# Second expert layer's weight tiles divided into four and three products, with buffers for each, in a fused attention and two-layer kernel

## The chip, the cores and the metric

The kernel runs on one core of a Trainium2 chip. The metric is the device time of one execution in microseconds (us), lower is better. Three runs of the kernel before are shown, and one further execution was profiled.

## The reference, cut to what matters

Causal attention with a bias from cumulative sums, then two expert layers. The second of these is the one the change touches: `x` is 2304 tokens of 512 numbers, `w_in` 512 x 2048, `w_out` 2048 x 512.

```python
attn_out = _attn_ref(q, k, v, s)                    # 4 batches, 8 heads, 576 tokens, 64 wide
x = attn_out.transpose(0, 2, 1, 3).reshape(B * S, H * D)
x = (x @ w_a) * (x @ w_b) @ w_out                   # first expert layer, 512 -> 1536 -> 512
h = x @ w_in                                        # second expert layer
r = np.maximum(h, 0.0)
return (r * r) @ w_out
```

## The kernel before

**Order.** Python code traces the whole program as operations with costs and dependences, and the class `Plan` (lines 73 to 261) sorts them: it keeps a clock for each engine and for the DMA queue and gives each engine the operation that can start first, ties by a rank. A tile's buffers belong to a tag with a fixed count (`Tag`); a tile can start when a buffer of its tag is free. So a change of tags or sizes in one place moves operations of every engine from the first point on at which such a tile matters. All operations are issued at line 261 (line 256 for fillers), so the trace is read by tile names, not by lines. All loads and stores are issued by SP, in the planned order; a DMA that waits holds up those behind it on SP.

**Numbers.** Each matrix product of 32-bit numbers is made of three matmuls: a high part (`..h`) times high, low times high, high times low. A tile pair (`z` = 0, 1) holds high and low words of a weight.

**Stages.** Attention and the first expert layer run together until about 380 us; the first layer then goes on by chunks (tiles `ab`, `py`), and its last chunk of 768 tokens, `wide` (lines 1174 to 1314, tiles `wa`, `wb`, `wc`, `pw`), uses seven products of 2 x 2 blocks in place of eight. The second layer works that way throughout: for each of three groups of 768 tokens (`t0`) and each of eight pairs of blocks (`j`, `PAIRS`) `first` (lines 1351 to 1426) makes the seven products, named `b11`, `b21`, `b22`, `t1` to `t4`, each six matmuls of 128 x 384, in the banks `a`, `b` and `c` (tiles `pa`, `pb`, `pc`). Its order is b11 in bank a, b21 in b, t2 onto a, t1 in c, t3 onto a, t4 onto a, b22 onto c. Between the products that add onto bank a ScalarE copies the bank out (`keep`, tiles `1..`, `2..`, `3..`, the copy before t2, t3, t4). `second` (lines 1448 to 1537, tiles `po`) multiplies the squares with the second matrix's tiles `ws` of 512 KB; the planner mixes both.

**The weights of `first`.** `split_in` (line 931) prepares seven combinations of the first matrix for each pair `j` and stores them to DRAM as `w2q[j][z]`, 128 rows of seven words of `QW` = 256 numbers, in the order of `SEVEN` (line 867). `first` loads both tiles whole, 896 KB each, and `times` picks a product's word by its place in `SEVEN`:

```python
def block(nm):
    return gated("lop", [P, 7, QW], F32R, "wq", 4, nm)
...
w = [block(f"w{nm}_{z}") for z in range(2)]
for z in range(2):
    dma(w[z].rearrange("p q c -> p (q c)").bitcast(F32), w2q[j][z], 896)
```

The tag `wq` has four buffers of 7168 bytes per partition, two pairs' worth. The same tag lends its first 4096 bytes to the sums `ws` of `wide` (line 1196) and, at the very end, to four of the seven last tiles `ws` of `second` (line 1455, products t3, t2, t4, b21 of `ENDING`); the other last tiles, b11, b22 and t1, use the three buffers of tag `lo`.

Of the kernel before, what the change touches and what calls it, by code (L numbers as in the profile page):

```python
# [7 lines left out]
F32 = mybir.dt.float32  # L8
F32R = mybir.dt.float32r
# [7 lines left out]
P = 128  # L17
# [246 lines left out]
def attention_moe_moe(tc, q, k, v, s, w_a, w_b, w_out, w_in2, w_out2, out):  # L264
    nc = tc.nc
    B, H, D, S = q.shape
    DM, NT = out.shape
# [33 lines left out]
    pl = Plan(nc)  # L301
# [15 lines left out]
    def pool(name):  # L317
        return lambda: pools[name]

    def gated(name, shape, dtype, tag, bufs, nm):  # L320
        return pl.tile(pool(name), shape, dtype, tag, bufs, nm, swapped)

    def sb(shape, dtype, tag, bufs, name):
        return pl.tile(pool("sb"), shape, dtype, tag, bufs, name)
# [4 lines left out]
    def scratch(shape, dtype, name):  # L329
        return pl.fixed(lambda: pools["dram"].tile(shape, dtype, name=name))  # L330

    def mm_bank(name):
        return pl.tile(pool("mm"), [P, 512], F32, "mm", 3, name)
# [5 lines left out]
    def matmul(out, n, pairs, start=True, lag=0.0):  # L339
        more = {} if start else {"skip_group_check": True}  # L340
        calls = [
            ("matmul", (out, a, b), {"start": start and i == 0, "stop": i == len(pairs) - 1, **more})
            for i, (a, b) in enumerate(pairs)
        ]
        cost = len(pairs) * (n / 2.4 + 13)
        pe(cost, calls, out, [x for pair in pairs for x in pair], lag)
# [19 lines left out]
    def dma(out, in_, kb, takes=(), lag=0.0):  # L366
        pl.call(("SP", kb * 3.0, False, "dma_start", (out, in_), {}), takes=takes, lag=lag)
# [496 lines left out]

    PAIRS = NF2 // 2
    QW = 2 * P
    SEVEN = ["b11", "b21", "t4", "t2", "b22", "t3", "t1"]
    w2q = [[scratch([P, 7 * QW], F32, f"w2q{j}_{z}") for z in range(2)] for j in range(PAIRS)]

    def temp(dtype, nm):  # L870
        return gated("lop", [P, 2 * DM], dtype, "tmp", 4, nm)

    def block(nm):
        return gated("lop", [P, 7, QW], F32R, "wq", 4, nm)

    def combine(n, out, a, b, op=ALU.subtract):
        kw = {"out": out, "in0": a, "in1": b, "op": op}
        pl.call(on_gps("tensor_tensor", n, **kw), on_dve("tensor_tensor", n, two=True, **kw))
# [52 lines left out]
    def split_in(j, late=False):  # L931
        def send(j, names, both):
            l, n = SEVEN.index(names[0]), len(names) * QW
            for z, x in enumerate(both):
                dma(w2q[j][z][:, l * QW : l * QW + n].part(names[0]), x.bitcast(F32), 0.6 * n)
# [58 lines left out]
    def halves(nm, dtype):  # L994
        t = sb([P, 2 * W], dtype, "g", GB, nm)
        return [t[:, z * W : z * W + W].part(z) for z in range(2)]
# [164 lines left out]
    def product(ps, left, right, start=True):  # L1161
        xh, xl = right
        pairs = []
        for d in range(2):
            wh_, wl_ = (z[d] for z in left)
            pairs += [(wh_, xh[:, d]), (wh_, xl[:, d]), (wl_, xh[:, d])]
        matmul(ps, CW, pairs, start, 0.0 if start else STEP)
# [6 lines left out]
    def wide(c):  # L1174
# [17 lines left out]
        def sums(f):  # L1192
            nm = f"{c}_{f}"
            lo = sb([P, 2, ND, P], F32R, "lo", 3, f"lo{nm}")
            dma(lo.bitcast(F32), wlab[f], 512)
            ws = gated("lop", [P, 7 * QW], F32, "wq", 4, f"ws{nm}")[:, : 2 * DM]
            a11, a12, a21, a22 = (ws[:, i * QW : i * QW + QW].part(i // 2) for i in range(4))
            for i in range(2):
                combine(
                    DM, ws[:, i * DM : i * DM + DM].part(i), wh[f, i].rearrange("p d c -> p (d c)").bitcast(F32),  # L1200
                    lo[:, i].rearrange("p d c -> p (d c)").bitcast(F32), ALU.add,
                )
            combine(QW, a22, a21, a22, ALU.add)
            combine(QW, a21, a11, a21)
            combine(QW, a11, a22, a11)
            combine(QW, a12, a12, a11)
            left[f] = lo, ws
# [84 lines left out]
        for f in range(3):  # L1292
            sums(f)
# [42 lines left out]
    def urgent(f, *a, **kw):  # L1336
        was, pl.stream = pl.stream, "first"
        f(*a, **kw)
        pl.stream = was
# [11 lines left out]
    def first(t0, j, left, held):  # L1351

        nm = f"{t0}_{j}"
        pair = j % 2
        yq = y_quads[t0]
        w = [block(f"w{nm}_{z}") for z in range(2)]
        for z in range(2):
            dma(w[z].rearrange("p q c -> p (q c)").bitcast(F32), w2q[j][z], 896)

        def times(ps, q, start=True):  # L1360
            i = SEVEN.index(q)
            product(ps, [[x[:, i, d * P : d * P + P] for d in range(2)] for x in w], yq[q], start)

        def bank_(k):
            if t0 == 0 and j == 1:
                return gated("po", [P, 512], F32, "po", 5, f"p{k}{nm}")[:, :CW]
            return mm_bank(f"p{k}{nm}")[:, :CW]

        v1, v3 = (x[:, :CW] for x in halves(f"v{nm}a", F32))
        v2, v4 = (x[:, :CW] for x in halves(f"v{nm}b", F32))  # L1370

        def squared(v, ps, s):
            if s is None:
                urgent(act, "activation", CW, v, ps, AF.Relu, psum=True)
            else:
                urgent(dve, "tensor_tensor", CW, out=v, in0=ps, in1=s, op=ALU.add)
                pl.call(
                    on_act("activation", CW, v, v, AF.Relu),
                    on_dve("tensor_scalar_max", CW, v, v, 0.0, two=True, each=0.52),
                )  # L1380
            kw = {"out": v, "in0": v, "in1": v, "op": ALU.mult}
            pl.call(on_act("activation", CW, v, v, AF.Square), on_dve("tensor_tensor", CW, two=True, **kw))
            return v

        def split(q, v):
            if q in ROOM:
                if pair == 0:
                    held[q] = flat(ROOM[q], 1, f"g{nm}{q}")
                hi, lo = (held[q][:, 2 * pair + z, :CW].part((pair, z)) for z in range(2))
            else:  # L1390
                hi, lo = (flat("wh", 3 * NF1, f"g{nm}{q}{z}")[:, :CW] for z in range(2))
            left[q, pair] = hi, lo
            copy(CW, hi, v, by="A")
            subtract(CW, lo, v, hi.bitcast(F32))

        def keep(tag, bufs, width, k, ps):
            t = sb([P, width], F32, tag, bufs, f"{k}{nm}")[:, :CW]
            urgent(act, "copy", CW, t, ps, psum=True)
            return t

        a = bank_("a")
        times(a, "b11")
        s1 = keep("a", 2, 512, 1, a)
        b = bank_("b")
        times(b, "b21")
        b11 = squared(v1, b, s1)
        times(a, "t2", False)
        s2 = keep("lo1", 1, DM, 2, a)
        b = bank_("c")
        times(b, "t1")  # L1410
        times(a, "t3", False)
        s3 = keep("a", 2, 512, 3, a)
        b22 = squared(v3, b, s3)
        times(a, "t4", False)
        b21 = squared(v2, a, None)
        times(b, "b22", False)
        b12 = squared(v4, b, s2)
        split("b11", b11)
        split("b22", b22)
        split("b21", b21)  # L1420
        combine(CW, b22, b22, b12)
        combine(CW, b12, b12, b11)
        combine(CW, b11, b11, b22, ALU.add)
        combine(CW, b21, b21, b11)
        for q, v in (("t3", b22), ("t1", b12), ("t2", b11), ("t4", b21)):
            split(q, v)
# [21 lines left out]
    def second(t0, grp, left, q, d):  # L1448

        nm = f"{t0}_{grp}{q}"  # L1450
        last = grp == PAIRS // 2 - 1
        end = last and t0 + 2 * CW >= NT
        if d == 0:
            if end and ENDING.index(q) > 2:
                wt = block(f"ws{nm}")[:, :4].rearrange("p (a b) c -> p a b c", a=2)
            else:
                wt = sb([P, 2, 2, QW], F32R, "lo", 3, f"ws{nm}")
            streamed[nm] = wt
            src = w2s[grp][OUT.index(q)]
            pl.add(  # L1460
                {"SP": (1536.0, [("dma_start", (wt.bitcast(F32), src), {})], False)},
                [wt], [src.part((q, i, z)) for i in range(2) for z in range(2)],
            )
        wt = streamed[nm]
        stays = q in STAYS
        if not stays:
            ps = mm_bank(f"po{nm}{d}") if end and (ENDING.index(q) + d) % 2 else gated("po", [P, 512], F32, "po", 5, f"po{nm}{d}")
        elif grp == 0:
            if (q, d) == (STAYS[0], 0):
                ps = mm_bank(f"po{nm}{d}")  # L1470
            else:
                ps = gated("po", [P, 512], F32, "po", 5, f"po{nm}{d}")
            banks_[q, d] = ps
        else:
            ps = banks_[q, d]
        ps = ps[:, :CW]
# [14 lines left out]
        x = {k: (lambda k: lambda: home(t0, k, d))(k) for k in ORDER}  # L1491
# [108 lines left out]
```

## Time and profile before

| | |
|---|---|
| median of 3 runs | 1021.84 us (1020.78 to 1024.65) |
| profiled execution, its own time | 1023.91 us |
| its span in the trace | 1022.1 us |
| TensorE matmuls busy | 1002.8 us, 98% |
| VectorE, ScalarE, GpSimd busy | 72%, 59%, 32% |
| DMA | 240.58 MB, mean 235 GB/s |
| loads of `w` | 48 of 896 KB, median 6.7 us to landing |

How to read it: a busy share near 100% on one engine means that only what lets that engine stand still can move the time. PE is TensorE's matmuls, PEld its weight loads, DVE VectorE, ACT ScalarE, POOL GpSimd, SP the engine that issues the DMAs. Idle time is read as the length of a stretch less the busy time in it, and the list of waits tells which instruction ended it.

### The profile page before, as it was taken

How to read it: one execution, taken by the hardware profiler on the slowest of the kernel's cores; microseconds unless marked ns; L12 is line 12 of the kernel's file. 1: busy time of each engine (PE TensorE's matmuls, PEld its weight loads, DVE VectorE, ACT ScalarE, POOL GpSimd, SP SyncE). 2: the span in 40 equal slices, each digit the busy share in tenths (PEclk: the TensorE clock that was granted, in tenths of full speed). 3: DMA queues.
4: the chain of work that ended last, by engine and by line, in shares of the span. 5: the costliest groups of instructions: out<-in, count | busy, mean ns of one | idle time of the engine just before them, and what ended most of it. 6: DMA issues, size and time to landing. Idle time of an engine off the chain costs nothing.

```text
span 1022.1 us, 16764 instructions
## 1 busy us (share of the span) xinstructions
PE 1002.8 (98%) x5612; PEld 867.8 (85%) x5619; DVE 735.5 (72%) x1546; ACT 603.9 (59%) x1373; POOL 322.3 (32%) x293
## 2 busy tenths in 40 slices
PE   9999999999999999999999999999999999999997
PEld 5766777777777778788889999999999999999997
DVE  5878876756677765565697898688767755876566
ACT  6777886565777643343344544487565766657552
POOL 2243134325454622101122323323335212431123
PEclk9999999999999999999999999999999999999999
DMA  7458896558778667857666668499968876678664
GB/s 226 131 157 256 273 288 186 152 150 258 228 199 246 185 212 262 275 183 233 206 207 207 208 206 273 164 336 363 344 219 322 313 260 231 246 273 319 220 233 165
DMA packets 138006, 240.58 MB, mean 235 GB/s; under 512 B 21320, under 2 KB 91072, under 8 KB 137920
## 3 DMA queue, kind: packets, MB, share of 16 engines
q1 hardware_dynamic: 137920, 239.52, 71.1%
q8 instruction: 44, 0.72, 0.3%
q14 instruction: 42, 0.34, 0.1%
HBM read 181.42 MB, written 52.11 MB: 228 GB/s over the span
## 4 chain that ended last, share of the span: by engine, by line
PE 75%; DMA 5%; DVE 2%; SPq 1%; ACT 1%; issue 0%; DVEq 0%; ACTq 0%
PE ab L261 14%; PE pa L261 9%; PE py L261 8%; PE po_0t L261 6%; PE pw L261 5%; PE pc L261 5%; PE wa L261 4%; PE st L261 3%; PE av L261 3%; PE pt L261 3%; PE wc L261 2%; PE pb L261 2%; PE po_2b L261 2%; PE po_1b L261 2%; PE po_0b L261 2%; PE po_3b L261 2%
## 5 line engine op out<-in xcount | busy, mean ns | idle before, releaser
L261 ACT ACTIVATE e<-st,neg 120x336 f32<-120x336 f32 (+2 forms) x192 | 93.5, 492 | 28.5 <-DVE neg L261 26.6
L261 PE MATMUL py<-g,wh 128*128 128x512 f32 x288 | 92.0, 401 | 1.4 <-DVE y L261 1.2
L261 PE MATMUL ab<-xh,wh 128*128 128x512 f32 x192 | 77.4, 403 | 0.0
L261 PE MATMUL ab<-xh,lo 128*128 128x512 f32 x192 | 75.0, 391 | 0.0
L261 PE MATMUL ab<-xl,wh 128*128 128x512 f32 x192 | 75.0, 390 | 0.0
L261 PE MATMUL pt<-ident,e 120*120 120x120 f32 (+2 forms) x480 | 68.0, 268 | 0.8 <-DVE ph L261 0.4
L261 PEld LDWEIGHTS pt<-ident,e 120*120 120x120 f32 (+2 forms) x480 | 51.2, 133 | 20.2 <-issue 9.2
L261 DVE CUSTOM_DVE_ANT_0 st<-st,mask 96x96 f32<-96x96 f32 (+4 forms) x120 | 53.7, 453 | 20.0 <-PE st L261 18.2
L261 PE MATMUL ab<-x,wh 128*128 128x512 f32 x192 | 65.8, 424 | 0.8 <-ACT a L261 0.7
L261 PEld LDWEIGHTS py<-g,wh 128*128 128x128 f32 x288 | 53.3, 190 | 12.6 <-DVE y L261 1.6
L261 PE MATMUL av<-ph,val 120*64 120x240 f32 (+3 forms) x512 | 58.7, 360 | 0.0
L261 PE MATMUL st<-fk,fq 65*120 65x336 f32 (+2 forms) x192 | 56.3, 408 | 1.7 <-ACT e L261 1.7
L261 ACT COPY ph<-pt 120x360 f32<-120x360 f32 (+3 forms) x81 | 36.5, 459 | 35.9 <-PE pt L261 34.8
L261 PE MATMUL py<-g,loo 128*128 128x512 f32 x144 | 56.9, 395 | 0.0
L261 PEld LDWEIGHTS av<-ph,val 120*64 120x64 f32 (+1 forms) x512 | 31.1, 136 | 24.9 <-issue 12.4
L261 DVE COPY ph<-pt 120x360 f32<-120x360 f32 (+3 forms) x79 | 39.8, 514 | 16.2 <-PE pt L261 14.9
L261 DVE TENSOR_TENSOR ab<-ab,a 128x512 f32<-128x512 f32 x36 | 25.2, 701 | 33.3 <-PE ab L261 28.7
L261 PEld LDWEIGHTS ab<-xh,lo 128*128 128x128 f32 x192 | 36.0, 188 | 7.7
L261 ACT COPY a<-ab 128x512 f32<-128x512 f32 x36 | 21.1, 586 | 35.7 <-PE ab L261 35.6
L261 PEld LDWEIGHTS ab<-xh,wh 128*128 128x128 f32 x192 | 36.1, 188 | 6.4 <-issue 0.4
L261 PEld LDWEIGHTS ab<-x,wh 128*128 128x128 f32 x192 | 33.7, 189 | 9.2 <-ACT a L261 1.6
L261 PEld LDWEIGHTS ab<-xl,wh 128*128 128x128 f32 x192 | 36.2, 188 | 5.9
(692 smaller groups left out, 3098.4 us busy)
## 6 DMA issues: line engine op xcount, KB each, us to landing
w<-w2q SPq DMA_DIRECT2D x48, 896.0 KB, 6.7
lo<-wlab SPq DMA_DIRECT2D x36, 512.0 KB, 4.7
w2q<-w2ip SPq DMA_DIRECT2D x48, 256.0 KB, 4.2
w2s<-w2op SPq DMA_DIRECT2D x48, 256.0 KB, 4.6
loo<-wlo SPq DMA_DIRECT2D x24, 384.0 KB, 5.5
w2ir<-in_moe_w_in SPq DMA_DIRECT2D x16, 512.0 KB, 5.7
w2or<-in_moe_w_out SPq DMA_DIRECT2D x16, 512.0 KB, 4.3
ws_0t<-w2s SPq DMA_DIRECT2D x12, 512.0 KB
```

Source lines behind the costliest of these rows:

```text
L261: getattr(eng, method)(*map(real, args), **{k: real(a) for k, a in kw.items()})
```

## The change

`SEVEN` is put in another order: b11, b21, t3, t1, then t4, t2, b22. A `w` tile is no longer loaded whole: words 0 to 3 go into a tile of tag `wq4` (512 KB), words 4 to 6 into one of tag `wq3` (384 KB), each tag with four buffers, together as many bytes as before. `times` takes its word from the half that holds it. The sums of `wide` and the last tiles of `second` use `wq4`. There are 96 loads of `w` in place of 48, and each waits only for the stores of its own words. The number and shapes of the matmuls stay.

```diff
-    SEVEN = ["b11", "b21", "t4", "t2", "b22", "t3", "t1"]
+    SEVEN = ["b11", "b21", "t3", "t1", "t4", "t2", "b22"]
+    NEAR = 4
...
-    def block(nm):
-        return gated("lop", [P, 7, QW], F32R, "wq", 4, nm)
+    def block(nm, n=NEAR):
+        return gated("lop", [P, n, QW], F32R, f"wq{n}", 4, nm)
...
-            ws = gated("lop", [P, 7 * QW], F32, "wq", 4, f"ws{nm}")[:, : 2 * DM]
+            ws = gated("lop", [P, 2 * DM], F32, f"wq{NEAR}", 4, f"ws{nm}")
...
-        w = [block(f"w{nm}_{z}") for z in range(2)]
-        for z in range(2):
-            dma(w[z].rearrange("p q c -> p (q c)").bitcast(F32), w2q[j][z], 896)
+        w = {}
+        for c0, n in ((0, NEAR), (NEAR, 7 - NEAR)):
+            for z in range(2):
+                w[c0, z] = block(f"w{nm}_{c0}{z}", n)
+                src = w2q[j][z][:, c0 * QW : (c0 + n) * QW]
+                pl.add(
+                    {"SP": (n * 384.0, [("dma_start", (w[c0, z].rearrange("p q c -> p (q c)").bitcast(F32), src), {})], False)},
+                    [w[c0, z]], [src.part(x) for x in ("b11", "t3", "t4", "t2") if c0 <= SEVEN.index(x) < c0 + n],
+                )
...
             i = SEVEN.index(q)
-            product(ps, [[x[:, i, d * P : d * P + P] for d in range(2)] for x in w], yq[q], start)
+            c0 = i // NEAR * NEAR
+            product(ps, [[w[c0, z][:, i - c0, d * P : d * P + P] for d in range(2)] for z in range(2)], yq[q], start)
...
-                wt = block(f"ws{nm}")[:, :4].rearrange("p (a b) c -> p a b c", a=2)
+                wt = block(f"ws{nm}").rearrange("p (a b) c -> p a b c", a=2)
```

In the rows below a name like `w_3_1` is pair 3, low words; in the change `w_3_01` is pair 3, words from 0, low, and `w_3_40` words from 4, high; the last number is the tile's own.

SP, the loads of pairs 2 and 3 for the first 768 tokens (`yd` stores the first layer's result, `ws_0b` are weights of `second`). Before:

```order
L261 DMA w_2_0_7358<-w2q_0_3969 128x1792
L261 DMA w_2_1_7364<-w2q_1_3997 128x1792
L261 DMA yd_7274<-yo_3_7402 128x512
L261 DMA yd_7274<-yo_4_7425 128x256
L261 DMA ws_0b_7445<-w2s_5673 128x1024
L261 DMA yd_7274<-yo_4_7425 128x256
L261 DMA yd_7274<-yo_5_7440 128x256 x2
L261 DMA w_3_0_7484<-w2q_0_4504 128x1792
L261 DMA w_3_1_7487<-w2q_1_4517 128x1792
```

The change:

```order
L261 DMA w_2_00_7349<-w2q_0_3969 128x1024
L261 DMA w_2_01_7358<-w2q_1_3997 128x1024
L261 DMA yd_7287<-yo_3_7368 128x512
L261 DMA w_2_40_7390<-w2q_0_3969 128x768
L261 DMA w_2_41_7395<-w2q_1_3997 128x768
L261 DMA ws_0b_7412<-w2s_5694 128x1024
L261 DMA yd_7287<-yo_4_7417 128x256
L261 DMA w_3_00_7443<-w2q_0_4504 128x1024
L261 DMA w_3_01_7459<-w2q_1_4517 128x1024
```

Pair 3's first four words now stand two stores further ahead; its last three follow behind the stores.

TensorE, pair 2 of the same tokens, where product t3 ends. Before:

```order
L261 MATMUL pa_2_7450<-t3h_7245,w_2_0_7358 128x384
L261 MATMUL pa_2_7450<-t3l_7268,w_2_0_7358 128x384
L261 MATMUL pa_2_7450<-t3h_7245,w_2_1_7364 128x384
L261 MATMUL pa_2_7450<-t4h_7272,w_2_0_7358 128x384
L261 MATMUL pa_2_7450<-t4l_7289,w_2_0_7358 128x384
```

The change:

```order
L261 MATMUL pa_2_7434<-t3h_7262,w_2_01_7358 128x384
L261 MATMUL pa_3_7538<-b11h_7132,w_3_00_7443 128x384
L261 MATMUL pa_3_7538<-b11l_7143,w_3_00_7443 128x384
L261 MATMUL pa_3_7538<-b11h_7132,w_3_01_7459 128x384
L261 MATMUL pa_3_7538<-b11h_7132,w_3_00_7443 128x384
L261 MATMUL pa_3_7538<-b11l_7143,w_3_00_7443 128x384
L261 MATMUL pa_3_7538<-b11h_7132,w_3_01_7459 128x384
L261 MATMUL pa_2_7434<-t4h_7295,w_2_40_7390 128x384
```

Product b11 of pair 3 has moved between t3 and t4 of pair 2. The opposite happens in `wide`, block 8, where before `pw` and the product b21 stood between b11 and t2, and now t2 follows b11 at once.

SP, the last loads of the program (`ws_2t` and `ws_3..` are the last tiles of `second`; with the product's name in them). Before:

```order
L261 DMA ws1536_2t2_11011<-w2s2_6707 128x1024
L261 DMA ws1536_2t4_11056<-w2s2_6707 128x1024
L261 DMA ws1536_3b11_11111<-w2s3_7531 128x1024
L261 DMA ws1536_3t4_11139<-w2s3_7531 128x1024
L261 DMA ws1536_3b21_11142<-w2s3_7531 128x1024
L261 DMA ws1536_3b22_11153<-w2s3_7531 128x1024
L261 DMA ws1536_3t1_11176<-w2s3_7531 128x1024
```

The change:

```order
L261 DMA ws1536_2t2_11107<-w2s2_6738 128x1024
L261 DMA ws1536_2t4_11152<-w2s2_6738 128x1024
L261 DMA ws1536_3t4_11200<-w2s3_7563 128x1024
L261 DMA ws1536_3b21_11202<-w2s3_7563 128x1024
L261 DMA ws1536_3b11_11211<-w2s3_7563 128x1024
L261 DMA ws1536_3b22_11249<-w2s3_7563 128x1024
L261 DMA ws1536_3t1_11272<-w2s3_7563 128x1024
```

The tiles for t4 and b21 have moved ahead of the one for b11. On TensorE half of product t3's work (6 of 12 matmuls), which stood between b11's and b22's use, has moved behind t1's.

## Rows read from the trace of the kernel before

**Rows 1.** The page's head: span, and each engine's busy time, share and instructions.
```profile
span 1022.1 us, 16764 instructions
...
PE 1002.8 (98%) x5612; PEld 867.8 (85%) x5619; DVE 735.5 (72%) x1546; ACT 603.9 (59%) x1373; POOL 322.3 (32%) x293
```

**Rows 2.** By stretch: length, PE, PEld, DVE, ACT, POOL busy, clock, DMA, GB/s.
```profile
0.00:400.00 400.00, 391.73 (x2282) 289.83 (x2289) 288.09 (x777) 270.56 (x715) 153.99 (x145) 1.00 0.70 212
400.00:500.00 100.00, 99.95 (x443) 81.88 (x443) 59.25 (x93) 36.67 (x62) 11.01 (x12) 1.00 0.72 234
500.00:600.00 100.00, 97.77 (x528) 89.62 (x527) 83.66 (x147) 46.81 (x82) 25.88 (x24) 1.00 0.65 208
600.00:680.00 80.00, 80.00 (x458) 76.35 (x457) 63.53 (x110) 43.48 (x84) 25.52 (x20) 1.00 0.68 228
680.00:700.00 20.00, 18.36 (x103) 17.40 (x102) 17.31 (x33) 15.53 (x35) 6.84 (x7) 1.00 1.03 386
700.00:740.00 40.00, 39.43 (x227) 38.90 (x226) 31.75 (x60) 23.38 (x52) 13.39 (x13) 1.00 0.95 343
740.00:850.00 110.00, 109.57 (x630) 108.81 (x629) 75.00 (x132) 69.11 (x144) 33.42 (x28) 1.00 0.76 274
850.00:900.00 50.00, 49.13 (x284) 48.81 (x283) 37.92 (x59) 32.40 (x66) 20.94 (x17) 1.00 0.68 248
900.00:1000.00 100.00, 100.00 (x579) 100.00 (x578) 64.36 (x117) 63.33 (x132) 21.87 (x21) 1.00 0.73 258
1000.00:1010.00 10.00, 9.14 (x53) 8.82 (x52) 7.03 (x12) 2.62 (x6) 5.21 (x5) 1.00 0.56 206
1010.00:1022.10 12.10, 7.71 (x45) 7.39 (x43) 7.63 (x14) 0.00 (x0) 4.22 (x4) 0.95 0.36 130
```

**Rows 3.** Waits of PE from 640 us on: total us, times, longest.
```profile
PE po_3b L261 <- DMA ws_3b<-w2s: 0.9, 1, 0.9
PE pa L261 <- ACT 30_2_7535 L261: 0.6, 1, 0.6
...
PE pa L261 <- DMA w<-w2q: 0.4, 1, 0.4
```

**Rows 4.** Timeline of PE: start, us, instruction, [idle before <- what ended it].
```profile
680.80 0.34 PE L261 MATMUL pa<-t3h,w 128*128 128x384 f32 x1
681.76 0.44 PE L261 MATMUL pa<-t4h,w 128*128 128x384 f32 x1 [0.62 <-ACT 30_2_7535 L261]
...
684.92 0.62 PE L261 MATMUL pa<-b11h,w 128*128 128x384 f32 x2 [0.45 <-DMA w<-w2q]
```

**Rows 5.** The chain that ended last: start, us, what.
```profile
677.25 7.63 DMA w<-w2q
...
1000.23 6.76 DMA ws_3b<-w2s
```

**Rows 6.** Timeline of SP, the end: issues of second-layer weights.
```profile
995.79 0.32 SPq L261 DMA_DIRECT2D ws_3b<-w2s  x1
...
999.11 1.49 SPq L261 DMA_DIRECT2D ws_3b<-w2s  x2
```

**Rows 7.** Timeline of PE, the end.
```profile
1001.84 0.68 PE L261 MATMUL po_3b<-g_6b,ws_3b 128*128 128x384 f32 x3
...
1007.03 2.35 PE L261 MATMUL po_3b<-g_6b,ws_3b 128*128 128x384 f32 x12 [0.86 <-DMA ws_3b<-w2s]
```

**Rows 8.** DMA issues: count, KB each, median us to landing.
```profile
w<-w2q SPq DMA_DIRECT2D x48, 896.0 KB, 6.7
lo<-wlab SPq DMA_DIRECT2D x36, 512.0 KB, 4.7
```

**Rows 9.** Timeline of SP: loads of `yrx` and `w`.
```profile
432.09 3.00 SPq L261 DMA_DIRECT2D yrx<-xd  x6
...
624.82 1.54 SPq L261 DMA_DIRECT2D w<-w2q  x3
```

**Rows 10.** Instructions of tile `w` on SP, 676 to 740 us.
```profile
L261 SPq DMA_DIRECT2D w<-w2q x10: 319/398/1072, 676.8 to 731.7; - x10
```

## The prediction

> **What bounds the kernel now.** I read the head of the page first: TensorE's matmuls are busy 1002.8 of 1022.1 us, 98% [rows 1]. The change adds and removes no matmul, so all it can give or take is the time in which TensorE stands still after the point from which the order of work differs, about 500 us. The table by stretch says how much that is: the span of a stretch less PE busy. From 500 to 600 it is 100.00 - 97.77 = 2.23 us, then 0, 1.64, 0.57, 0.43, 0.87, 0 and 0.86 us up to 1010 us [rows 2]: **6.6 us in all**. The 4.4 us of the last stretch are mostly the last addition and the last store, which the change leaves as they are. The last column but one is the DMA engines' share: from 680 to 700 us they are full (1.03, 386 GB/s), from 700 to 740 us nearly (0.95); in the rest of this half about a quarter or more is free [rows 2].
>
> Then the list of waits, for the last third: what ended TensorE's idle time [rows 3]. Three waits of about 0.6 us are for ScalarE (one is shown), one of 0.9 us for a tile of the last layer's second half (`ws_3b`), and **one of 0.4 us for the weight tiles that the change divides**. That is the whole direct claim of `w` on TensorE in 48 loads. The timeline shows both kinds [rows 4]: at 681.76 us product t4 waits until ScalarE has copied the bank that t3 left at 680.80, and at 684.92 us product b11 of the next pair of blocks waits for its load. Its load is in the chain of waits: issued at 677.25, landed 7.63 us later [rows 5].
>
> **The change, part by part.**
>
> *The divided tiles at 684 us.* Before, both tiles of pair 3 wait for the last of seven products (b22) of pair 1, and 2 x 896 KB have to land before b11. Now b11 needs only two tiles of 512 KB, and these follow the last of b11, b21, t3, t1 of pair 1. By the order of TensorE, seven products lie between that point (t3 of pair 1) and b11 of pair 3: b11, b21 of 2, t4, b22 of 1, t2, t1, t3 of 2, each of 6 matmuls, 100 us / 579 = 0.173 us apart in the stretch from 900 us [rows 2], 1.04 us, in all 7.3 us. Landing: 7.63 us, less the 768 KB that no longer come first, at 386 GB/s 2.0 us, gives 5.6 us. The tile of second-layer weights and the two 384 KB tiles of pair 2 that stand ahead in SP's order, 1280 KB, could add up to 3.4 us, 9.0 us. I take 5.6, since the old landing already had such a neighbour: the wait goes, **-0.45 us**. Bounds -0.45 and +1.2 (9.0 less 7.3, less the old 0.45).
>
> *ScalarE's copies.* Where two products of one bank stand side by side and a copy of the bank lies between them, TensorE waits 0.6 us [rows 3, 4]. The order has three such places before (t3 to t4 of pairs 2 and 3, t2 to t3 of pair 4), which are the three waits. In the changed order the two of pairs 2 and 3 are parted by other products; pair 4 now has t2, t3, t4 in one run, two places; and one is new in the first layer's wide part, b11 and t2 of block 8. Three against three: **0.0 us**. Bounds -0.6, if the new one is covered, and +0.6, if ScalarE is later there.
>
> *The end.* The last tiles of second-layer weights for t4 and b21 go into the pool of the four-product tiles, which come free after t3 of the last pair and no longer after b22. SP therefore issues these two, 1 MB, before the tile for b11, and no longer after it. The tile for b22 has to wait for the same release as before (issued 1000.23 us, landed 6.76 us later [rows 5], the second of the two issues from 999.11 [rows 6]); before, a 512 KB load stood right ahead of it, and TensorE waited 0.86 us [rows 7]. Now nothing does, but the order puts only 6 instead of 12 matmuls between b11's use and b22's, so it is due 1.04 us sooner, 4.8 us after its issue. Loads of 512 KB land in 4.7 us as a median [rows 8] and landed 6.76 us after issue here. With 4.7 the wait is 0 (-0.86), with 6.8 it is 2.0 us (+1.1). Near the middle, 5.5 us, it is 0.7: **-0.2 us**. The tile for b11, issued at 995.79 [rows 6] and due at about 1001.84 [rows 7], now shares the engines with the two loads ahead of it; the upper bound holds its wait too.
>
> *Loads moved and added.* The three-product tiles of pairs 0 and 1 no longer queue for a buffer that the wide part holds. In SP's order these four loads, 1.5 MB, now stand among the six loads of `yrx` of 432.09 us, where the first whole tiles went out at 624.82 us [rows 9]. What covers them is 100 us in which TensorE is idle for 0.05 us and the DMA engines have 0.28 of their time free [rows 2]. Cost 0; without that cover it would be 1.5 MB at 386 GB/s, 4 us, put on the load of `lo` behind them. SP issues 48 DMAs more, 0.4 us each (the middle one of the three times in ns [rows 10]), 19 us in 390 us: 0, as long as nothing queued behind them is late. A half tile's wait for its buffer holds up the second-layer weights (`ws`) queued behind it on SP, and TensorE waits for those; in steady work they wait for products at about the same place of TensorE's order, so I price that at 0 too and leave its risk to the bounds of the next part.
>
> *The rest of the 6.6 us* (6.6 - 0.45 - 1.8 - 0.86 = 3.5 us: waits for VectorE, for banks and one more for a load) depends on which engine the schedule gives a piece to. I have no row for the new neighbours; I take it as unchanged, with bounds of all of it gone and as much again, -3.5 and +3.5 us.
>
> **Sum.** -0.45 + 0.0 - 0.2 = -0.65 us. Against the profiled execution, 1023.91 us (span 1022.1 and 1.8 us around it), that is 1023.3 us. That execution lay 2.07 us above the median of the runs shown, 1021.84, so the median should come to **1021.2 us**. A measurement of this kernel tells about 0.5%, 5.1 us, from no change; nothing in the sum comes near that.
>
> **Rivals.**
>
> *DMA becomes the bound from 680 to 740 us (slower).* Ten loads of `w`, 9.2 MB, are issued between 676 and 740 us [rows 10], where the engines have little room. At 386 GB/s they take 23.8 us. If the smaller pieces cost the engines more, I take the rate of the stretches with smaller and mixed loads, 212 GB/s at 0.70, or 303 GB/s at a full share [rows 2]: 30.4 us, 6.6 us more, with 0 to 2 us of room (5% of 40 us). It decides as soon as the rate falls so far that the excess outgrows those 2 us, at about 356 GB/s. Taken whole it gives 1021.84 + 6.6 = 1028.4 us. For it: the shares of 1.03 and 0.95. Against it: loads of 512 KB land in 4.7 us and of 896 KB in 6.7 us [rows 8]; a straight line through the two leaves some 2 us that don't grow with size, but 386 GB/s [rows 2] over a landing time of 6.7 us is 2.6 MB, nearly three such loads in flight at once, so that part lies beside other loads. Chance 0.10.
>
> Beside it: the Trainium skill, DMA: Bandwidth & Descriptors (Anatomy of one DMA, and Bandwidth), gives each DMA a fixed 2.0 us, advises batches of 1 MiB or more, and so speaks against this change. By that, as an estimate, ten more DMAs here would add 20 us if none overlapped. The trace agrees with the size of the fixed part and disagrees with adding it up.
>
> *All waits go (faster).* If loads that come sooner also let VectorE and ScalarE run ahead, the whole 6.6 us could close: 1021.84 - 6.6 = 1015.2 us. Against it: two of the three kinds of wait have nothing to do with loads. Chance 0.07.
>
> *The halves come no sooner.* SP issues in order, and a half tile stands behind the same loads as the whole one; then the 0.45 us stay and nothing moves: 1021.8 us. For it: one wait on `w` in all [rows 3]. Chance 0.20.
>
> **How the numbers follow.** The forecast, 1021.2 us, has 0.63. Its unknowns together, if most go one way: -3.5 and another -0.7 at the end give 1017.0; +1.65 (from -0.45 to +1.2), +1.3 (from -0.2 to +1.1), +0.6 and a third of the 3.5 give 1026. The range **1017.0 to 1026.0** holds the third rival, and leaves out the first two, 0.17. Faster by over 0.5% (under 1016.7) 0.07; slower (over 1026.9) 0.11, the first rival and a tail of the forecast; the same 0.82.
>
> **What would show it.** Right: PE busy again about 1002.8 us; no wait for `w` near 684 us; three waits for ScalarE of 0.6 us, one of them in the wide part (500 to 650 us) and two on pair 4; at the end one wait for `ws_3b` of 0 to 2 us; loads of `w` of 512 and 384 KB landing in under 6.7 us. Wrong: idle time of TensorE in 680 to 740 us above 4 us, ended by DMA; waits near 440 us for `lo`; or waits for VectorE and banks, between 500 and 1010 us, that have grown from 3.5 to over 7 us.

## The result, and the profile after

The changed kernel takes **1026.75 us** (median of 12 executions, 1023.86 to 1031.38) against 1020.56 us for the kernel before (1016.45 to 1024.65): ratio **1.006, interval 1.004 to 1.008**. That is 6.2 us slower, past the top of the predicted range, 1026.0 us.

The same views as before, first the table by stretch from 500 to 740 us; the columns are those of [rows 2].

```profile
500.00:600.00 100.00, 93.53 (x492) 85.47 (x491) 77.30 (x137) 41.03 (x72) 28.82 (x28) 0.98 0.60 200
600.00:680.00 80.00, 79.42 (x454) 75.19 (x453) 62.34 (x102) 39.25 (x71) 28.36 (x23) 1.00 0.64 207
680.00:700.00 20.00, 19.65 (x114) 18.95 (x113) 18.46 (x38) 17.62 (x39) 5.91 (x5) 1.00 1.01 356
700.00:740.00 40.00, 38.80 (x220) 37.67 (x219) 32.79 (x66) 25.96 (x57) 11.34 (x11) 1.00 1.00 361
```

Read it against [rows 2]. Up to 500 us TensorE's idle time is as before. From 500 to 600 us TensorE stands still for 6.47 us where it was 2.23 us, and the granted clock is 0.98 and no longer 1.00. In the stretches that the divided tiles were made for, 680 to 740 us, idle time went from 2.21 to 1.55 us. (Fixed stretches hold slightly other work after the change, since the second layer starts 7.8 us later.) The list of waits says who ended the idle time from 500 us on; its first lines:

```profile
PE wc L261 <- DVE wx L261: 4.6, 1, 4.6
PE pc L261 <- DVE v_0a L261: 1.7, 2, 0.9
PE pw L261 <- DVE gl L261: 1.5, 2, 1.1
PE wa L261 <- ACT s1w L261: 0.6, 1, 0.6
PE pa L261 <- ACT 30_4_7895 L261: 0.6, 1, 0.6
PE pa L261 <- ACT 20_4_7875 L261: 0.6, 1, 0.6
PE po_3b L261 <- DMA ws_3b<-w2s: 0.4, 1, 0.4
...
```

No line for `w` is left, the three waits for ScalarE are there and the last load costs 0.4 us: all as forecast against [rows 3]. The loss is in the first line, one single wait of 4.6 us for `wx`, the mixed weights of block 0 of `wide`. TensorE's timeline there:

```profile
514.53 0.34 PE L261 MATMUL wc<-t1lx,wx 128*128 128x384 f32 x1
519.51 1.01 PE L261 MATMUL wc<-t1hx,wx 128*128 128x384 f32 x2 [4.64 <-DVE wx L261]
520.32 0.53 PE L261 MATMUL wc<-t1lx,wx 128*128 128x384 f32 x1
520.64 0.53 PE L261 MATMUL wc<-t1hx,wx 128*128 128x384 f32 x1
```

The first two matmuls of product t1 use the high words of `wx`, which ScalarE has copied; the third needs the low words, which VectorE subtracts. After the wait the matmuls start 0.32 us apart and no longer 0.174 us; the table over these three microseconds has the granted clock at 0.50, the lower of the two levels (1.2 GHz), right behind 4.7 us in which TensorE was busy for 0.07 us:

```profile
514.80:519.50 4.70, 0.07 (x1) 0.00 (x0) 4.70 (x8) 1.66 (x2) 1.03 (x1) 0.97 0.16 56
519.50:522.50 3.00, 2.99 (x9) 2.99 (x10) 3.00 (x6) 0.00 (x0) 0.00 (x0) 0.50 0.01 3
```

Why is `wx` late? VectorE's timeline before:

```profile
510.68 0.70 DVE L261 TENSOR_TENSOR ab<-ab,a 128x512 f32<-128x512 f32 x1 [1.04 <-PE ab L261]
...
511.75 1.23 DVE L261 TENSOR_TENSOR wx<-ws,wx 128x1024 fp32r<-128x1024 f32 x1
```

and after:

```profile
511.95 0.70 DVE L261 TENSOR_TENSOR ab<-ab,a 128x512 f32<-128x512 f32 x1 [1.16 <-PE ab L261]
512.56 0.99 DVE L261 TENSOR_TENSOR ws<-wh,lo 128x512 f32<-128x512 f32 x1
...
514.57 1.54 DVE L261 TENSOR_TENSOR ws<-ws 128x256 f32<-128x256 f32 x1
516.03 0.68 DVE L261 TENSOR_TENSOR ws<-wh,lo 128x512 f32<-128x512 f32 x1
...
517.57 0.75 DVE L261 TENSOR_TENSOR ws<-ws 128x256 f32<-128x256 f32 x2
518.24 1.21 DVE L261 TENSOR_TENSOR wx<-ws,wx 128x1024 fp32r<-128x1024 f32 x1
```

From 511.95 us on VectorE is busy without a break; it does the pieces `ws` of blocks 1 and 2, which TensorE does not need yet, ahead of the one that it waits for. The sums of block 0 are not what is late: ScalarE starts to copy them into `wx` 0.26 us behind block 0's first matmul in both kernels (at 510.41 and 511.68 us, shown below). Before:

```profile
510.67 1.05 ACT L261 CAST wx<-ws 128x1024 fp32r<-128x1024 f32 x1
```

and after:

```profile
511.94 1.05 ACT L261 CAST wx<-ws 128x1024 fp32r<-128x1024 f32 x1
```

The subtraction starts right behind that copy before, and 5.3 us behind its end after. What stands upstream is SP's timeline, where the four three-product tiles of pairs 0 and 1 go out in between the loads of `yrx`, which before followed each other [rows 9]:

```profile
433.36 1.85 SPq L261 DMA_DIRECT2D yrx<-xd  x4
435.25 2.06 SPq L261 DMA_DIRECT2D w<-w2q  x4
437.36 0.43 SPq L261 DMA_DIRECT2D yrx<-xd  x1
```

What comes before block 0 differs from run to run (its first matmul starts between 504.20 and 511.68 us in the table below), so it is taken out: below, times run from block 0's first matmul to the second layer's first, and from there to the end of the last matmul. Before:

```profile
510.41 0.33 PE L261 MATMUL wa<-b11hx,wh 128*128 128x384 f32 x1
...
654.16 0.33 PE L261 MATMUL pa<-b11h,w 128*128 128x384 f32 x1
...
1015.46 2.25 PE L261 MATMUL po_3b<-g_6b,ws_3b 128*128 128x384 f32 x12
```

After:

```profile
511.68 0.33 PE L261 MATMUL wa<-b11hx,wh 128*128 128x384 f32 x1
...
661.94 0.33 PE L261 MATMUL pa<-b11h,w 128*128 128x384 f32 x1
...
1022.70 2.07 PE L261 MATMUL po_3b<-g_6b,ws_3b 128*128 128x384 f32 x11
```

The part `wide` went from 143.75 to 150.26 us, **+6.5 us**; the second layer went from 363.55 to 362.83 us, **-0.7 us**. In sum +5.8 us. The two profiled executions themselves are 7.3 us apart (1031.21 and 1023.91 us), 1.3 us of which lie ahead of block 0; the medians are 6.2 us apart.

How the 6.5 us of `wide` divide into standing still and working more slowly is read from its length and TensorE's busy time in it, before and after:

```profile
510.41:654.16 143.75, 141.51 (x788) 132.30 (x787) 119.43 (x207) 65.55 (x118) 42.66 (x38) 1.00 0.66 213
511.68:661.94 150.26, 143.21 (x787) 133.73 (x786) 120.40 (x205) 64.42 (x116) 50.70 (x46) 0.99 0.60 195
```

Idle time grew from 2.24 to 7.05 us, **4.8 us**, and the same matmuls were busy for **1.7 us** more.

### The profile page after: what moved, and what is told of

The parts are those of the page before. It is cut to its first block, busy times and chain, and to the rows that moved or that the text cites. A ratio compares the mean times of both kernels' runs of the same rounds, so it can differ in the third digit from the quotient of the medians.

```text
span 1029.4 us, 16908 instructions
## 1 busy us (share of the span) xinstructions
PE 1005.8 (98%) x5619; PEld 870.5 (85%) x5619; DVE 736.6 (72%) x1548; ACT 596.5 (58%) x1360; POOL 334.6 (33%) x304
## 4 chain that ended last, share of the span: by engine, by line
PE 88%; DVE 4%; DMA 3%; issue 2%; POOL 1%; ACT 1%; SPq 0%; POOLq 0%; DVEq 0%
PE ab L261 17%; PE py L261 9%; PE pa L261 8%; PE st L261 7%; PE po_0t L261 5%; PE av L261 5%; PE pt L261 5%; PE pw L261 5%; PE wa L261 5%; PE pc L261 4%; PE wc L261 2%; PE pb L261 2%; PE po_1b L261 2%; PE po_2b L261 2%; PE po_0b L261 2%
```

## The experiments

Theory A: the four loads that now go out early make the planner write another order of VectorE's work ahead of block 0; the wait, and the low clock behind it, are the loss. Rival B: 96 smaller loads in place of 48 cost something everywhere. Other rivals came up on the way. This table holds all runs; the times of the three instructions are read from each trace as in the two fences above.

| kernel | ratio to before (interval) | block 0 | second layer | end | block 0 to end |
|---|---|---|---|---|---|
| before | 1 | 510.41 | 654.16 | 1017.71 | 507.3 |
| changed | 1.006 (1.004 to 1.008) | 511.68 | 661.94 | 1024.77 | 513.1 |
| e1_late | 1.0169 (1.0147 to 1.0191) | 508.83 | 652.37 | 1031.4 | 522.5 |
| e2_mix | 1.0226 (1.0201 to 1.0251) | 505.44 | 652.18 | 1032.1 | 526.7 |
| e5_loads | 1.0097 (1.0078 to 1.0117) | 505.38 | 656.23 | 1022.9 | 517.6 |
| e6_fill | 1.0044 (1.0026 to 1.0062) | 508.35 | 657.29 | 1019.5 | 511.1 |
| late_stores | 0.9974 (0.9953 to 0.9996) | 507.90 | 651.37 | 1014.15 | 506.3 |
| mix_stores | 1.0107 (1.0080 to 1.0135) | 505.84 | 655.06 | 1025.7 | 519.9 |
| after_stores | 1.0044 (1.0023 to 1.0065) | 508.11 | 659.57 | 1021.6 | 513.5 |
| before_stores | 0.9997 (0.9980 to 1.0014) | 504.26 | 647.78 | 1012.3 | 508.0 |
| unseen_loads | 0.9992 (0.9976 to 1.0008) | 504.20 | 647.94 | 1011.0 | 506.8 |
| words_only | 1.0001 (0.9983 to 1.0019) | 504.62 | 648.13 | 1012.1 | 507.5 |
| late_again | 0.9982 (0.9962 to 1.0002) | 507.63 | 651.22 | 1014.2 | 506.6 |

### The early loads put back

```diff
                     [w[c0, z]], [src.part(x) for x in ("b11", "t3", "t4", "t2") if c0 <= SEVEN.index(x) < c0 + n],
+                    lag=190000.0 if t0 == 0 and j < 2 and c0 == NEAR else 0.0,
```

> The changed kernel, but its four three-product tiles of pairs 0 and 1 of the first token group are put back behind the wide part, so that SP issues them after 600 us and no longer at 435 us; the division, the order of the products and all other loads stay. Theory A (the four early loads push the yrx loads back, VectorE's planned order in front of block 0 of the wide part turns over, and TensorE waits 4.6 us for wx and then runs some 9 matmuls at a lower clock): the wait for wx near 514 us falls from 4.64 us to under 0.5 us, idle time from 500 to 600 us goes back from 6.47 to 2 to 3 us, and the time is 1020 to 1021 us, ratio 0.998 to 1.001. Rival B (the 48 additional, smaller loads cost a little everywhere): the time stays at 1026 to 1027 us, ratio 1.005 to 1.007, with PE idle from 600 to 1010 us above 4 us.

1036.97 us: the wait for `wx` is gone and `wide` takes 143.54 us, as before; and yet it is far slower than either theory said. The loss sits in another place. TensorE's and SP's timelines at 690 us:

```profile
697.15 4.21 PE L261 MATMUL po_0b<-g_0b,ws_0b 128*128 128x384 f32 x12 [3.81 <-DMA ws_0b<-w2s]
705.15 4.20 PE L261 MATMUL po_0b<-g_0b,ws_0b 128*128 128x384 f32 x12 [3.79 <-DMA ws_0b<-w2s]
713.12 0.66 PE L261 MATMUL po_0t<-g_0t,ws_0t 128*128 128x384 f32 x1 [3.77 <-DMA ws_0t<-w2s]
```

```profile
701.39 0.33 SPq L261 DMA_DIRECT2D ws_0b<-w2s  x1
...
707.26 1.92 SPq L261 DMA_DIRECT2D yd<-yo  x4
709.38 0.32 SPq L261 DMA_DIRECT2D ws_0t<-w2s  x1
```

Load, use, load, use, one at a time: the tile of 701.39 is issued when the 12 matmuls that began at 697.15 have ended. Those 12 take 4.21 us, where at the end of the kernel before 12 take 2.25 us: behind the waits the granted clock is 0.50 (0.52 for the next 12) as above. The tag `lo` has three buffers; two hold the first layer's last two outputs (`yo`), whose stores the planner ranks as late work, and here it has put them at 707 us, behind the loads `yr` of the next tokens. In the changed kernel these stores go out at 681 and 682 us.

### VectorE's order alone

```diff
+        pl.stream = "first"
         mix(0)
+        pl.stream = "moe"
```

> The changed kernel with all its early loads, but the two operations that make block 0's mixed words (the copy and the subtraction, tile wx) get the first rank in the planner, so that the subtraction stands on VectorE before the sums of blocks 1 and 2 are through. Theory A, in the form that VectorE's order alone is the cost: wait for wx from 4.64 us to under 1 us, the low clock behind it gone, 1020.5 to 1022 us, ratio 1.000 to 1.0015. Rival C (what costs is that everything there is ready late, since b11, the first right operand, is split 4.5 us later): the order helps by no more than 2 us, and the time is 1024.5 to 1026 us. Rival B (more, smaller loads): 1026 to 1027 us.

1041.97 us. The same trap (waits for `ws_0b` and `ws_0t` of 13.4 us, stores at 708 us) hides what was asked. In the stretch from 500 to 600 us the wait for `wx` fell to 1.0 us, and the idle time from 6.47 only to 4.35 us, since waits for other results of VectorE stand there now (`y` 1.7 us, `s3w` 0.9 us).

### The early loads alone, without the division

```diff
+        rooms = [gated("lop", [P, 7 * QW], F32, "wq", 4, f"ws{c}_{f}") for f in range(4)]
         for f in range(3):
             sums(f)
+        for f in range(4):
+            src = w2q[f // 2][f % 2][:, 4 * QW :]
+            names = ("b11", "t3", "t4", "t2")
+            pl.add({"SP": (3 * 384.0, [("dma_start", (rooms[f][:, 2 * DM :], src), {})], False)},
+                   [rooms[f].part("x")], [src.part(x) for x in names])
...
-            ws = gated("lop", [P, 7 * QW], F32, "wq", 4, f"ws{nm}")[:, : 2 * DM]
+            ws = rooms[f] if f < 4 else gated("lop", [P, 7 * QW], F32, "wq", 4, f"ws{nm}")
+            ws = ws[:, : 2 * DM]
```

> The kernel before, undivided tiles and old order of products, with four additional loads of 384 KB at the place in SP's order where the changed kernel has its four early ones, into words of the ws tiles that nothing reads; the output is unchanged. VectorE's, ScalarE's and GpSimd's order in front of block 0 then is that of the changed kernel. Theory A: the loss appears without any division: a wait of 3 to 5 us for wx near 514 us, a lower clock behind it, 1025 to 1027 us, ratio 1.004 to 1.007. Rival B (division, not the early loads): 1020 to 1021 us, ratio 0.999 to 1.001, with no wait for wx above 0.5 us.

1029.37 us, above the range expected (1025 to 1027 us). Whole tiles, the old order of words, and the loss is there. The first of its waits and VectorE's row for the subtraction:

```profile
PE wc L261 <- DVE wx L261: 4.5, 1, 4.5
```

```profile
511.99 1.22 DVE L261 TENSOR_TENSOR wx<-ws,wx 128x1024 fp32r<-128x1024 f32 x1
```

`wide` takes 150.85 us, +7.1 us, much as in the changed kernel. Another 3.2 us went in the second layer (366.7 against 363.55 us), where the waits for `w` are 1.3 us and were 0.4 us; that part was not taken apart. Rival B falls: division is not needed for the loss.

### The wait filled with work

```diff
             product(b, w[6], xq["t1"])
+            if f == 0:
+                again = ("matmul", (b, w[1][0][0], xq["b21"][0][:, 0]), {"start": True, "stop": True})
+                pl.ops[-1].ways["PE"][1][:0] = [again] * 27
```

> The changed kernel with 27 additional matmuls of 128x384 on TensorE directly ahead of product t1 of block 0, on operands of the product before and into the bank that t1 then overwrites, so that TensorE works through the 4.64 us in which it stood still (27 x 0.173 us = 4.7 us). It computes the same. Theory A with its clock part (some 9 matmuls behind the wait take 320 ns and not 174 ns because TensorE stood still, 9 x 0.146 = 1.3 us): the steps behind t1's first matmul are 174 ns, the granted clock from 500 to 600 us is 1.00 and no longer 0.98, and the time is 1.0 to 1.5 us less, 1025.3 to 1025.8 us. Rival D (the low clock there comes from something else, or is no cost): steps of 320 ns remain, and the time is that of the changed kernel, 1026.7 us, or up to 0.3 us more.

1024.05 us. The additional matmuls with the row behind them, and the clock from 500 to 600 us (the third number from the right):

```profile
510.92 4.95 PE L261 MATMUL wc<-b21hx,wh 128*128 128x384 f32 x27 [0.30 <-DVE g L261]
515.71 0.33 PE L261 MATMUL wc<-t1hx,wx 128*128 128x384 f32 x1
```

```profile
500.00:600.00 100.00, 98.17 (x530) 90.41 (x529) 78.38 (x138) 41.41 (x75) 28.58 (x28) 1.00 0.60 197
```

The wait is full of work, nothing behind it runs at the lower clock, and `wide` takes 148.94 us, 1.3 us less than in the changed kernel. Rival D falls: the low clock goes with the standing still (the three profiles with the wait of 4.5 to 4.64 us, changed, e5_loads and after_stores, have it; this one does not). So of the 1.7 us that TensorE's matmuls in `wide` took longer, 1.3 us are the low clock. Of the 4.8 us of idle time `wx` is 4.6 us; the other waits nearly cancel (`s1w` 0.6, `g` 0.3 and `gl` 0.9 us came, `y` 1.2 and `s3w` 0.2 us went).

The trace shows this, the medians do not: the ratio of 1.0044 is also that of the changed kernel with one rank moved (after_stores below), which fills nothing, and the time lies below the range expected (1025.3 to 1025.8 us), taken beside runs of the kernel before with a median of 1019.04 us.

### The stores out of the way

Since e1_late and e2_mix fell into a second hole, the four stores of `yo` from tag `lo` get the first rank, in those two kernels and in both controls:

```diff
+                was, pl.stream = pl.stream, "first"
                 for z in range(2):
                     d = 2 * (i - ND) + z
                     dma(yd[c][d][:, W:].part((d, 1)), o[:, z * n : z * n + n], n * 0.5)
+                pl.stream = was
```

> The kernel of e1_late, in which the four early loads are held back, and besides the four stores of the first layer's last two outputs (yd from yo, tiles of the pool lo) get the first rank, so that SP issues them near 680 us as in the changed kernel and no longer at 707 us. Theory A2 (with the loads late, TensorE no longer waits for wx; what cost 16 us in e1_late is that these stores were put behind the yr loads, so that two of the three buffers of lo stayed full and the loads of ws_0b and ws_0t went through one buffer): waits for ws between 690 and 720 us fall from 11.4 us to under 2 us and the time is 1019 to 1021.5 us, ratio to before 0.998 to 1.0015. Rival E (the divided tiles let TensorE run ahead to the ws loads, whose landing then bounds it, stores or not): waits for ws above 6 us remain, 1028 to 1035 us.

1018.27 us, slightly better than any theory had it. The longest waits from 500 us on:

```profile
PE py L261 <- DVE y L261: 1.3, 1, 1.3
PE pc L261 <- DVE v_0a L261: 0.9, 1, 0.9
PE po_0t L261 <- DMA ws_0t<-w2s: 0.8, 1, 0.8
PE pw L261 <- DVE gl L261: 0.7, 1, 0.7
...
```

Those for `y`, `v_0a` and `gl` stand in the kernel before with 1.2, 0.9 and 0.7 us. No `wx`, and 0.8 us for `ws` where e1_late had 11.4. Rival E falls, and the stores are shown to be the 16 us of e1_late: 11.4 us of waits and, behind them, matmuls at the lower clock. This kernel has the whole division; what it lacks is only the four early loads.

> The kernel before with the first rank for the four stores and nothing else, the control. It issues them between 665 and 676 us already. Theory A2: no change, ratio 0.998 to 1.002. If the stores' rank is worth something by itself, faster than 0.998.

> The changed kernel with the first rank for the four stores and nothing else. Theory A2: it issues them at 681 and 682 us already and loses its time at 514 us, so nothing is to be had: the wait for wx stays at 4.5 us and the time is 1025.5 to 1027.5 us, ratio 1.005 to 1.007. Rival E, or any theory by which the stores cost the changed kernel its 6 us: 1020 to 1022 us.

The controls: 1020.55 us, ratio 0.9997, and 1025.29 us, ratio 1.0044 (0.2 us below the lower end expected; the wait for `wx` is 4.64 us). The stores' rank is worth nothing that can be told where the planner does not push them back. In after_stores `wide` takes 151.46 us, 1.2 us more than in the changed kernel behind the same wait: the granted clock stays at 0.50 until 521.40 us, 5.5 us from the end of the wait (515.94 us) and not 3.0.

> The kernel of e2_mix, with early loads and the first rank for block 0's mixed words, and the same first rank for the four stores. Theory A2: the wait for wx stays at about 1 us (e2_mix had 1.0) and the waits for ws fall from 13.4 us to under 2 us: 1020 to 1023 us, ratio 1.000 to 1.003. Rival E: waits for ws above 6 us, 1030 us or more. Rival C (all is ready late because b11 is split late): 1024.5 to 1026 us with no single wait over 1.5 us from 500 to 600 us.

1032.16 us: the time is in Rival E's range, but its waits are not. Those for `ws` fell from 13.4 to 5.1 us, more than theory A2 had (2 us) and less than Rival E (6 us). SP's timeline at the longest of them:

```profile
673.39 6.24 SPq L261 DMA_DIRECT2D w<-w2q  x4
...
683.88 0.44 SPq L261 DMA_DIRECT2D ws_0b<-w2s  x1
```

Four half tiles take 6.2 us to get through SP; 4.6 us of this is one wait until TensorE is done with a product in bank `c`. `ws_0b` stands behind them and some other issues, lands 8.3 us after its issue, and TensorE waits 2.97 us for it. How much of these 2.97 us the half tiles cost was not taken apart. From 500 to 600 us 4.40 us stay idle, 2.1 us less than in the changed kernel. So `wx` alone, moved up, gives back about half of the 4.2 us that this stretch had lost. `wide` takes 146.7 us in e2_mix and 149.2 us in mix_stores, between the 143.75 before and the changed kernel's 150.26. Its idle time is 4.4 and 4.5 us; the two differ by 2.4 us of busy time, and the granted clock tells why: behind the wait for `wx` it is 1.00 in e2_mix (wait of 0.99 us) and 0.58 in mix_stores (1.26 us, the mean of 3.9 us). Even at full clock some 3 us of the loss are left with `wx` in front, and no run tells whether the rest of VectorE's order or something that is ready late is behind them: Rival C stays open for that half.

### The planner's order or the traffic

```diff
-                    {"SP": (n * 384.0, [...
+                    {"SP": (0.0 if t0 == 0 and j < 2 and c0 == NEAR else n * 384.0, [...
```

> The kernel of after_stores, with its four early loads of 384 KB still issued among the yrx loads at 435 us, but the planner is told that these four move nothing, so that its order of the other engines' work is not turned over by them: block 0's mixed words stand ahead of the sums of block 2 again. Theory A2 (the order that the planner wrote is the cost, and not the 1.5 MB on the chip's queues): wait for wx under 1 us, idle time from 500 to 600 us 2 to 3.5 us, 1018 to 1021 us, ratio 0.997 to 1.000. Rival F (the 1.5 MB themselves hold up the yrx and lo loads, and whatever the order, wx is late): a wait of 2 to 5 us near 510 us remains, 1022 to 1026 us.

1018.53 us, with the early loads still on SP at the same place:

```profile
424.77 1.85 SPq L261 DMA_DIRECT2D yrx<-xd  x4
426.67 2.05 SPq L261 DMA_DIRECT2D w<-w2q  x4
```

and VectorE in the old order, `wx` ahead of the pieces of blocks 1 and 2:

```profile
505.54 1.60 DVE L261 TENSOR_TENSOR wx<-ws,wx 128x1024 fp32r<-128x1024 f32 x1 [0.28 <-ACT wx L261]
```

`wide` takes 143.74 us. The 1.5 MB move and cost nothing that can be told (ratio 0.9992); it was the order that the planner wrote when it counted them. Rival F falls.

### The words alone, and the best kernel again

> The kernel before with the changed order of the seven products' words in the tiles and nothing else; tiles stay whole. All theories: where a word lies in a tile costs nothing, ratio 0.998 to 1.002, no wait for wx; a time above 1.004 would put part of the loss on the order of the words.

1019.62 us, ratio 1.0001: the place of a word costs nothing that can be told.

> The kernel of late_stores once more, to see whether it beats the kernel before by more than a measurement can tell. By the terms of the prediction alone (0.65 us less) the ratio is 0.999 to 1.000; if its first ratio, 0.9974, is its own, it comes to 0.996 to 0.9985 again.

1018.36 us, ratio 0.9982, inside the second case, but its interval reaches 1.0002. Both runs together put the divided tiles with late loads and early stores some 0.2% below the kernel before; one of the two intervals lies wholly under 1, the other does not, so it is the best kernel here by a margin hardly larger than what can be told.

## Why the prediction was wrong

*The divided tiles at 684 us* (-0.45): right in the changed kernel. The list has no wait for `w` any more, and loads of 512 and 384 KB land in 4.7 and 5.7 us as medians. (The smaller take longer, so the straight line that the prediction drew through two sizes says little about a fixed part of a landing.) The margin is thin: in after_stores product b11 waits 0.48 us for `w` at 687.40 us again.

*ScalarE's copies* (0.0): right, three waits of 0.6 us before and after, at the places named, one in `wide` and two on pair 4. The one in `wide` belongs to the 6.5 us that this part lost, and was saved in the second layer.

*The end* (-0.2): right in kind, 0.39 us for `ws_3b` where 0.86 us were, so -0.5.

Together with the rest of the second layer that part gained 0.7 us, where the terms had summed to 0.65. That these agree is luck: the load, the ScalarE wait that moved to `wide` and the end make -1.55 us there, and new waits, for `v_0a` above all (1.7 us, was 0.9), took about half of it back.

*Loads moved and added* (0): **this step failed**; the runs put 6.5 us of `wide` in its place. It priced the four early loads by what they could delay, the load of `lo` and TensorE's 100 us of cover, and as traffic they cost nothing indeed (unseen_loads). But the planner's clock of the DMA queue counts them too. Behind them it placed `yrx` later, and from there it chose other engines and another order for every piece of work whose turn was close. The section on the kernel before says that a change of tags moves operations of every engine, and the one on the change looks at the order in three places; the place 75 us behind the early loads, where VectorE's order decides, was not one of them. That the planner's order is the cost is shown (unseen_loads, late_stores); that the place of `wx` on VectorE is about half of it is shown too (e2_mix, mix_stores); which part of the order makes the other half stays open.

*The rest of the 6.6 us* (3.5 us, bounds of 0 and 7): this is the term that grew. Idle time from 500 to 1010 us is 6.47 + 0.58 + 0.35 + 1.20 + 0.86 + 0.87 + 0 + 0.39 = 10.7 us; less the three ScalarE waits and `ws_3b`, 8.5 us are left, above the bound of 7 and over what the list of wrong signs named. And a cost that no bound held came on top: 1.3 us at the lower clock right behind the wait, since the bounds counted a wait by its length only. The prediction's first premise, that with the same matmuls only TensorE's idle time can change, fails here: its busy time came to 1005.8 us and not again to 1002.8, 1.7 us of it in `wide`.

The rivals: the DMA engines did not become the bound (idle 1.55 us from 680 to 740 us), the waits did not all go, and the halves did come sooner (no wait for `w` is left). The slower side was given 0.11 for that and a tail; it came true by a mechanism that had no place among the rivals. The risk that a half tile holds up `ws` on SP was named and priced at 0. No wait for `ws` by this way is in the changed kernel's list, but half tiles that waited for buffers stand ahead of the load behind 2.97 us in mix_stores, so 0 hung on the order and is not a property of the change.

The rule of the Trainium skill weighed there (DMA: Bandwidth & Descriptors, Bandwidth: batches of 1 MiB or more) speaks against dividing. The figures of the Trainium skill there, the fixed 2.0 us too, are measured on DMAs that GpSimd issues; here SP issues all. By that rule late_stores, with 96 loads under that size, should lose; the trace disagrees at this size and load, ratios 0.9974 and 0.9982.

## What to carry to other kernels

Where a planner or scheduler writes the order, price a moved load by the first place where engines' choices are close, and compare the order of every engine there up to the next point where the bound engine waits, not only at the place the change is for. A buffer count that frees a load early is itself a change of order: hold the load back, or keep it out of the planner's account, and the intended gain can be seen by itself. And look for tiles that sit full until a low-ranked store goes out, for they turn three buffers into one.

## What the runs showed that was not expected

Standing still can cost more than its length, and not the same each time. Behind the wait of 4.64 us the granted clock was 0.50 for 3.0 us in the changed kernel and for 5.5 us in after_stores; behind waits of about 1 us at the same place it stayed at 1.00 in e2_mix and fell in mix_stores. The price was 0 to 2.5 us. Filling the gap with 27 matmuls that compute nothing new made `wide` 1.3 us shorter in the one profile taken.

The hole of 16 us (e1_late) was opened by removing a cause of delay. Four stores put 25 us later made three loads of 512 KB run one at a time, some 8 us apart, with 3.8 us of waiting for each and 4.2 us for the 12 matmuls between two, which take 2.25 us at full clock.

One piece `ws` on VectorE took 1.54 us where such pieces take 0.42 us as a median:

```profile
L261 DVE TENSOR_TENSOR ws<-ws x38: 408/418/1540, 499.6 to 635.6; 128x256 f32<-128x256 f32 x38
```

It starts at 514.57 us, 0.02 us behind an operation of GpSimd:

```profile
514.55 1.28 POOL L261 TENSOR_TENSOR w2ot<-w2ot,w2or 128x512 int32<-128x512 int32 x1 [0.18 <-POOL ws L261]
```

and ends 0.28 us after it, as if it had waited for it to finish; 1.1 us of the 4.6 us lie there. It is not alone: in the traces before and after seven pieces of this shape start while a GpSimd operation runs, and all seven end 0.28 to 0.29 us behind it; seven others start first, have a GpSimd operation start beside them, and take 0.41 to 0.42 us. The Trainium skill (SBUF — State Buffer, SBUF: two separate sides) has a pair of ports that a VectorE operation with two inputs from SBUF and a GpSimd operation that reads SBUF take in turn, each for its whole length; these rows agree, though no run here took the GpSimd operation away.
